# A written-out order of five engines replaced by another, with idle products at the beginning

## The chip, the cores and the metric

One core of a Trainium2 chip runs the kernel. The time is the device time of one execution in microseconds, here as the median of 11 runs. The core has a matrix engine (PE, with its weight loads shown apart as PEld), a vector engine (DVE), an activation engine (ACT), a general engine (POOL) and a queue engine (SP) that issues the large transfers. The engines run side by side, each through its own queue in order.

## The reference, cut to what matters

Four batches with 8 heads, 768 positions and 64 channels go through a decaying linear attention, and the result, as 3072 rows of 512, through a highway layer.

```python
for b in range(nb):                                  # blocks of 64 positions
    intra = np.einsum('bhic,bhjc->bhij', qb, kb) * Dmask[None]
    intra = np.einsum('bhij,bhjd->bhid', intra, vb)
    inter = np.einsum('bhid,bhde->bhie', qb * lam_pow[None], kv_state)
    out[:, :, sl] = intra + inter
    kv_state = lam_block * kv_state + np.einsum('bhsd,bhse->bhde', kb_dec, vb)
...
H = np.maximum(x @ w_h, 0.0)
T = 1.0 / (1.0 + np.exp(-(x @ w_t + b_t)))
return T * H + (1.0 - T) * x
```

## The kernel before, in words

The work is cut into 12 steps of 256 positions of one batch, numbered n = 0 to 11, three to a batch; each step has two halves b of 128 positions. The decay is put into q and v ahead of time (`pow_q`, `pow_v`), so that blocks of 128 positions need only a triangular mask, and the state `kv` stays in the accumulators of PE through the three steps of a batch.

Nothing is scheduled by a tool. `PLAN` is a string of tokens; each token calls one function of `DO` (line 350), and the functions issue their instructions in the order of the tokens. So the string sets the order of every engine's queue at once. After `@` stands the engine of a copy or scaling, after `=` the accumulator banks that a product writes. The tokens, with n the step:

- `Lq Lk Lv` (line 173, on SP): load of one half of the heads of q, k or v, a quarter MB each. `W.w.g` (line 178, SP): half of the weights w, half a MB. `WC` casts a quarter of a weight matrix.
- `CQ CK CV` (lines 191 and 105 or 103): scaling or cast of q, k, v to bf16. The last index is the half of the heads, or 2 for all of them.
- `TQ TK` (line 205, PE): eight transposes (four for one half of the heads). `EQ EK`: their copy to `qT` and `kT`.
- `S`, `U` and, woven together, `SS` (lines 217 and 222, PE): scores and the update of the state. The third index of `SS` is the half e. In the last step of a batch `SS.n.0` holds scores only. `M` (line 256, DVE): a mask of scores, four a step. `KE`: copy of the state to `ss`.
- `I` and `A` (lines 272 and 282, PE): output from the state and from the masked scores. `D`: its copy to `xT`.
- `F.i.u.w` (line 301, PE): products of token group i with half u of weight matrix w, eight matmuls of 256 columns. Groups 11 and 12 are the two halves of step 11, of 128 columns. `H` (line 306, DVE) and `G` (line 315, ACT) work on the two results, `X` (line 319, DVE) joins them.
- `R` (line 328, PE) turns the result back and adds x, `E` copies it out, `ST` (line 338, SP) stores it. `B` and `BC` transpose and copy the bias.
- `Z.r` (line 344): r products of the identity with itself into a bank that nobody reads. The plan before has none.

Buffers are named pools with a fixed number of turns (`BUFS`, line 64), and a load waits for the last reader of the buffer that it takes.

## Time and profile before

| | |
|---|---|
| median of 11 runs | 112.2 us (110.93 to 113.71) |
| the profiled execution, its own time | 111.49 us |
| its span, first to last instruction | 109.8 us |
| PE busy | 94.2 us, 86% of the span |
| DVE busy | 84.0 us, 77% |
| ACT busy | 65.8 us, 60% |
| POOL busy | 60.9 us, 55% |
| mean transfer rate over the span | 251 GB/s |

A line of a timeline shows the start, the length, the engine, the line of the kernel, the operation with its output and input, the count, and in brackets how long the engine had been idle and what released it. Several instructions of one line in a row are merged. A line of the chain of waits shows the start, the length and who held the chain. The busy time of PE is modelled at the ends of matmuls, so a share of 99% means that the next instruction always stood ready, not that the array was full.

### The profile page before, as it was taken

What the parts mean: (1) busy time and instruction counts of PE and PEld (TensorE: products, weight loads), DVE (VectorE), ACT (ScalarE), POOL (GpSimd) and SP (SyncE); (2) the same over time, 40 slices, a digit from 0 to 9 for tenths busy, and PEclk for the clock granted to TensorE, in tenths of its full rate; (3) what the DMA queues carried; (4) which work ended last, traced back from release to release, by engine and by line L of the source; (5) the groups of instructions that cost most, each with busy time, mean ns of one, the idle gap of its engine ahead of it and who ended that gap; (6) DMA issues with size and microseconds to landing.
All of it is one profiled execution on the core that took longest, in us unless ns stands there. A gap on an engine that the chain in (4) does not pass through costs nothing.

```text
span 109.8 us, 4558 instructions
## 1 busy us (share of the span) xinstructions
PE 94.2 (86%) x1969; PEld 82.6 (75%) x1969; DVE 84.0 (77%) x144; ACT 65.8 (60%) x120; POOL 60.9 (55%) x51
## 2 busy tenths in 40 slices
PE   0007887979999999999999999999999999999960
PEld 0005775848788888999978988888888888889950
DVE  0204796569795899799999899899989867867870
ACT  3581035622599947695346459619595739666970
POOL 6073797648489877979637679794638400000000
PEclk9999999999999999999999999999999999999999
DMA  0999999999999999999999999899985432020585
GB/s 4 267 293 288 290 295 327 322 321 322 281 275 305 288 282 298 283 294 317 318 319 304 301 294 314 272 349 323 308 264 198 155 122 75 0 96 0 188 309 178
DMA packets 43899, 27.55 MB, mean 251 GB/s; under 512 B 1764, under 2 KB 40936, under 8 KB 43880
## 3 DMA queue, kind: packets, MB, share of 16 engines
q1 hardware_dynamic: 43728, 27.27, 86.2%
q8 instruction: 15, 0.25, 1.0%
q14 instruction: 4, 0.03, 0.1%
q10 hardware_dynamic: 152, 0.01, 0.1%
HBM read 20.98 MB, written 6.29 MB: 248 GB/s over the span
## 4 chain that ended last, share of the span: by engine, by line
PE 51%; DMA 18%; SPq 14%; POOL 5%; DVE 5%; issue 2%; ACT 1%; DVEq 0%; POOLq 0%
PE bt L301 15%; SPq L173 13%; PE bh L301 12%; DMA kf<-in_k_dram 11%; DMA w_f<-in_moe_w_h_dram 7%; PE bx L328 6%; PE bs L217 5%; PE bo L282 3%; PE bktr L205 3%; POOL kb L105 3%; PE bo L272 3%; DVE hm L306 2%; PE bqtr L205 2%; POOL qb L191 2%; PE kv L222 1%
## 5 line engine op out<-in xcount | busy, mean ns | idle before, releaser
L301 PEld LDWEIGHTS <-w_b 128*128 128x128 bf16 x416 | 36.7, 98 | 5.8 <-POOL w_b L105 0.8
L256 DVE TENSOR_TENSOR m<-bs,tri 128x512 bf16<-128x512 f32 x48 | 31.0, 680 | 3.2 <-PE bs L217 2.9
L191 POOL TENSOR_TENSOR qb<-qf,pow_q 128x1024 bf16<-128x1024 f32 (+1 forms) x13 | 22.9, 1771 | 8.1 <-DMA qf<-in_q_dram 3.9
L315 ACT ACTIVATE bt<-bt,bt_col 128x256 f32<-128x256 f32 (+1 forms) x52 | 21.9, 430 | 8.4 <-PE bt L301 5.6
L301 PE MATMUL bh<-xT,w_b 128*128 128x256 bf16 (+1 forms) x208 | 24.6, 264 | 0.3 <-DVE w_b L105 0.3
L301 PE MATMUL bt<-xT,w_b 128*128 128x256 bf16 (+1 forms) x208 | 24.2, 265 | 0.1
L191 POOL TENSOR_TENSOR vs<-vf,pow_v 128x1024 bf16<-128x1024 f32 (+1 forms) x12 | 22.0, 1835 | 3.9 <-DMA vf<-in_v_dram 3.9
L319 DVE TENSOR_TENSOR th<-bt,hm 128x512 bf16<-128x512 f32 (+1 forms) x26 | 16.6, 644 | 2.9 <-ACT bt L315 2.0
L105 POOL CAST kb<-kf 128x1024 bf16<-128x1024 f32 (+1 forms) x12 | 12.0, 1003 | 10.8 <-DMA kf<-in_k_dram 8.3
L103 ACT ACTIVATE o<-bx 128x512 f32<-128x512 f32 x20 | 11.8, 597 | 9.2 <-PE bx L328 9.1
L306 DVE SCALAR_TENSOR_TENSOR hm<-bh,xT 128x512 bf16<-128x512 f32 (+1 forms) x26 | 16.2, 640 | 1.3 <-PE bh L301 1.3
L205 PE MATMUL bqtr<-id,qb 128*128 128x128 bf16 x96 | 8.2, 235 | 8.8 <-POOL qb L191 8.8
L217 PE MATMUL bs<-qT,kT 64*64 64x128 bf16 x384 | 14.6, 226 | 0.3 <-DVE qT L105 0.3
L217 PEld LDWEIGHTS <-kT 64*64 64x64 bf16 x384 | 11.4, 110 | 3.1 <-issue 2.1
L103 ACT ACTIVATE qT<-bqtr 128x1024 bf16<-128x1024 bf16 x9 | 9.2, 1027 | 7.6 <-PE bqtr L205 7.6
L205 PEld LDWEIGHTS <-qb 128*128 128x128 bf16 x96 | 6.2, 105 | 9.5 <-POOL qb L191 9.0
L328 PE MATMUL bx<-id,th 128*128 128x128 bf16 x96 | 12.9, 219 | 0.3 <-DVE th L319 0.3
L328 PE MATMUL bx<-id,xT 128*128 128x128 bf16 x96 | 12.9, 219 | 0.0
L103 ACT ACTIVATE xT<-bo 128x512 bf16<-128x512 f32 x13 | 9.2, 744 | 5.2 <-PE bo L282 5.2
L222 PE MATMUL kv<-vs,kb 64*64 64x64 bf16 x320 | 9.6, 201 | 0.9 <-ACT ss L103 0.8
L328 PEld LDWEIGHTS <-th 128*128 128x128 bf16 x96 | 9.4, 98 | 0.6 <-DVE th L319 0.5
L205 PE MATMUL bktr<-id,kb 128*128 128x128 bf16 x96 | 8.4, 235 | 1.4 <-POOL kb L105 1.3
(43 smaller groups left out, 102.6 us busy)
## 6 DMA issues: line engine op xcount, KB each, us to landing
qf<-in_q_dram SPq DMA_DIRECT2D x24, 256.0 KB, 5.2
kf<-in_k_dram SPq DMA_DIRECT2D x24, 256.0 KB, 5.5
vf<-in_v_dram SPq DMA_DIRECT2D x24, 256.0 KB, 5.5
out_dram<-o SPq DMA_DIRECT2D x23, 256.0 KB, 3.6
w_f<-in_moe_w_h_dram SPq DMA_DIRECT2D x2, 512.0 KB, 7.0
w_f<-in_moe_w_t_dram SPq DMA_DIRECT2D x2, 512.0 KB, 7.6
out_dram<-oh SPq DMA_DIRECT2D x2, 128.0 KB, 1.9
lam_bc<-in_lam_dram ACTq DMA_DIRECT2D x1, 4.0 KB, 3.5
```

Of the source, the lines that this page charges most:

```text
L103: A.activation(dst, src, AF.Copy)
L105: ENG[eng].tensor_copy(dst, src)
L173: nc.sync.dma_start(out=new((x + "f", n), [128, H, J * D], F32)[:, hs], in_=SRC[x][b, hs, c * 2 * C:(c + 1) * 2 * C, :].rearrange("h (p j) ...
L191: ENG[eng].tensor_tensor(dst, in0=get(src, n)[:, heads(p)].rearrange("p h (j d) -> p h j d", j=J), in1=pw[:, n % NST, heads(p), :, None].t ...
L205: T.transpose(t[:, i, j, :], get(x + "b", n)[:, j, h:h + 2, :], id128)
L217: T.matmul(get("s", n, e, hp // 2)[half(b), hp % 2, j, :], lhsT=get("kT", n)[half(e), hp, j, half(b)], rhs=get("qT", n)[half(e), hp, :, ha ...
L256: V.tensor_tensor(new(("m", n, e, u), [128, 2, J, C]), in0=get("s", n, e, u), in1=tri[:, None].to_broadcast([128, 2, J, C]), op=ALU.mult)
L301: T.matmul(t[:, r, :], lhsT=w_b[w][:, kc, (2 * u + r) * 128:(2 * u + r + 1) * 128], rhs=get("xT", *g)[:, kc, :], start=(kc == 0), stop=(kc ...
L306: V.scalar_tensor_tensor(new(("hm", g, u), [128, 2, z * C], tag=f"hm{z}"), in0=get("h", g, u), scalar=0.0, in1=get("xT", *g)[:, 2 * u:2 * ...
L315: A.activation(dst[:, r, :], src[:, r, :], AF.Sigmoid, bias=bt_col[:, 2 * u + r:2 * u + r + 1])
L319: ENG[eng].tensor_tensor(new(("th", g), [128, NP, z * C], tag=f"th{z}")[:, 2 * u:2 * u + 2, :], in0=get("tt", g, u), in1=get("hm", g, u), ...
L328: T.matmul(t[:, a * 128:(a + 1) * 128], lhsT=x[:, j, r * C:(r + 1) * C], rhs=id128, start=(a == 0 and i == 0), stop=(i == 1), skip_group_c ...
```

## The change

The string is replaced as a whole. The function `load` gets an argument for its queue; no token of the new string sets it. All work tokens are there as before; 55 of them have another engine, and nine `Z` tokens with 101 products in all are added. The start of the two strings:

```diff
-Lq.0.0 Lq.0.1 Lq.1.0 Lk.0.1 Lv.0.1 Lk.0.0 Lv.0.0 Lk.1.0 CQ.0.1@POOL Lq.1.1 Lv.1.1 CQ.0.0@POOL CK.0.1@ACT Lk.1.1
-TQ.0.0=0 TQ.0.1=1 Lv.1.0 TK.0.1=2 EK.0.1@DVE CK.0.0@POOL Lq.2.1 CV.0.1@DVE TK.0.0=3 EQ.0.1@DVE CV.0.0@POOL Lk.2.0
-EQ.0.0@DVE S.0.1=45 EK.0.0@DVE Lq.2.0 U.0.0 S.0.0=62 B=1 KE.0.0@DVE CQ.1.2@POOL W.0.1 M.0.1.0 U.0.1 M.0.0.1 Lk.2.1
-M.0.0.0 CK.1.2@POOL TQ.1.2=0 KE.0.1@DVE I.0=32 W.0.0 EQ.1.2@ACT CV.1.2@POOL TK.1.2=4 M.0.1.1 Lv.2.0 EK.1.2@DVE A.0.1
...
+Lk.0.0 Lk.0.1 Lk.1.0 Lq.0.0 Lv.0.0 Lv.0.1 Lq.0.1 Lk.1.1 Z.27=0 B=0 CK.0.1@ACT Lq.1.1 CK.0.0@ACT Z.2=1 TK.0.1=1 Lq.1.0
+TK.0.0=2 CQ.0.0@POOL Lv.1.1 EK.0.0@DVE BC CV.0.0@DVE Lv.1.0 Z.15=3 TQ.0.0=3 CV.0.1@DVE Lq.2.1 EQ.0.0@DVE Z.17=0 U.0.0
+CQ.0.1@POOL Lq.2.0 S.0.0=45 KE.0.0@DVE CK.1.2@ACT Lk.2.1 EK.0.1@DVE Z.9=0 U.0.1 M.0.1.0 TQ.0.1=6 Lk.2.0 TK.1.2=2
+M.0.0.0 EQ.0.1@ACT CQ.1.2@DVE W.0.1 EK.1.2@ACT Z.2=0 I.0=03 S.0.1=15 A.0.0 KE.0.1@ACT M.0.1.1 Z.4=4 TQ.1.2=6 Lv.2.0
+CV.1.2@DVE EQ.1.2@ACT W.1.1 M.0.0.1 Z.18=2 SS.1.1=42 CQ.2.2@POOL Lv.2.1 A.0.1 KE.1.0@ACT M.1.1.1 D.0.1@ACT M.1.1.0
+Z.7=1 SS.1.0=56 W.1.0 I.1=12 KE.1.1@ACT M.1.0.1 TQ.2.2=3 CK.2.2@ACT M.1.0.0 W.0.0 A.1.1 D.0.0@DVE A.1.0 WC.0.1.0@POOL
...
-    def load(x, n, p):
+    def load(x, n, p, eng):
...
-        nc.sync.dma_start(out=new((x + "f", n), [128, H, J * D], F32)[:, hs],
+        (A if eng else nc.sync).dma_start(out=new((x + "f", n), [128, H, J * D], F32)[:, hs],
```

In the order of each engine: K is loaded first instead of Q. CK of steps 0, 1 and 2 is on ACT; CQ.1.2 and all CV of steps 0 to 2 are on DVE; CQ of steps 0 and 2 stays on POOL. Of the weights, W.0.1 still comes first, then W.1.1, W.1.0 and W.0.0 (before: W.0.0, W.1.1, W.1.0). PE begins with Z.27 and has Z.15 and Z.17 ahead of TQ.0.0 and U.0.0, and runs the highway blocks of groups 0 and 1 in the order F.0.1.0, F.1.1.0, SS.2.0, F.0.1.1, F.1.1.1, SS.2.1, F.1.0.1, F.0.0.1 (before: F.0.1.0, F.0.0.0, F.1.1.0, F.1.0.0, SS.2.0, SS.2.1, F.0.1.1, F.1.1.1, F.0.0.1, F.1.0.1). On DVE the ramp reads EK.0.0, BC, CV.0.0, CV.0.1, EQ.0.0, KE.0.0, EK.0.1, M.0.1.0, M.0.0.0, CQ.1.2, M.0.1.1, CV.1.2, M.0.0.1, the four M of step 1, D.0.0, D.1.1, D.1.0, WC.1.1.1, H.1.1, CV.2.2; later come four masks, H.0.1, D.2.1, X.1.1, H.1.0, X.0.1, X.1.0, H.0.0, H.2.1, X.0.0, EQ.3.2. On ACT 15 of the 20 KE now stand (before 10). At the end E.10.0.2 and E.11.1.1 are on ACT instead of DVE.

## The prediction

> **What bounds the kernel now.** I read the busy table first, then busy time by stretches, the chain that ended last, and the timelines of the engines up to 29 us.

> ```profile
> span 109.8 us, 4558 instructions
> PE 94.2 (86%) x1969; PEld 82.6 (75%) x1969; DVE 84.0 (77%) x144; ACT 65.8 (60%) x120; POOL 60.9 (55%) x51
> ...
> PEclk9999999999999999999999999999999999999999
> ```
> ```profile
> 8.37:17.36 8.99, 7.48 (x129) 6.48 (x133) 6.34 (x12) 1.22 (x2) 6.44 (x5) 1.00 1.18 294
> 17.36:23.35 5.99, 4.50 (x144) 3.60 (x135) 3.21 (x8) 4.06 (x6) 3.95 (x4) 1.00 1.14 325
> 23.35:102.94 79.59, 79.00 (x1656) 69.62 (x1657) 70.32 (x115) 52.37 (x98) 46.59 (x31) 1.00 0.85 247
> 102.94:109.80 6.86, 3.26 (x56) 2.92 (x53) 3.23 (x8) 3.31 (x9) 0.00 (x0) 0.98 0.68 250
> ```

> The columns are stretch, length, then busy time of PE, its weight loads, DVE, ACT and POOL. From 23.35 PE is busy 79.0 of 79.6 us, so in that stretch PE's own work is the time and no new order can take much out. What can move is the ramp, 23.35 us that hold only about 8 us of PE work at full pace, and the tail, 6.86 us. DVE is second in the long stretch: 70.3 of 79.6 us, 88%.

> The ramp ends on a transfer. In the chain:

> ```profile
> 14.88 7.96 DMA w_f<-in_moe_w_h_dram
> 22.84 0.05 issue
> 22.90 0.88 POOL w_b L105
> 23.82 1.27 PE bh L301 x11
> ```

> The second block of weights lands at 22.8, is cast, and F.0.0.0 follows. Loads run in one queue, and the instructions that wait for them show the pace: the 4th load is used at 7.93 (CK.0.1 on ACT), the 6th at 9.77 (CK.0.0), the 9th at 12.44 (CQ.1.2), the 15th at 17.98 (CQ.2.2): 0.9 us per quarter MB, the n-th at 4.3 + 0.9n.

> PE is not at one speed, though the PEclk row never shows less than 9:

> ```profile
> 14.40 1.03 PE L205 MATMUL bqtr<-id,qb 128*128 128x128 bf16 x8 [0.47 <-POOL qb L191]
> 15.23 0.63 PE L272 MATMUL bo<-qT,ss 128*128 128x128 bf16 x4
> 15.65 1.06 PE L205 MATMUL bktr<-id,kb 128*128 128x128 bf16 x8
> 16.65 0.96 PE L282 MATMUL bo<-m,vs 64*64 64x128 bf16 x32
> ...
> 19.94 0.62 PE L205 MATMUL bqtr<-id,qb 128*128 128x128 bf16 x8
> ```

> The same eight transposes take 1.03 us at 14.40 and 0.62 at 19.94; less the 0.2 us of the last one's own time that is 107 ns apiece against 56. PE is slow until about 17.4, after 3.0 us of unbroken work since 14.40; it had begun steady work at 11.31, 6.1 us before, with a gap of 0.47.

> **The change, part by part.** The new argument of load() is empty in all 72 load tokens, so every load stays on SP. What changes is the order on each queue, the engine of 55 evacuations and casts, and 101 idle products.

> *Idle products.* Z.27 needs only id128, ready at 1.4: 27 x 107 ns = 2.9 us, 1.45 to 4.35. Real work can't start before ACT has loaded its tables (7.56) and cast K: CK.0.1 0.63 us, so TK.0.1 at 8.25 and TK.0.0 at 8.8 to 9.25. Z.15 then stands before TQ.0.0 and Z.17 before U.0.0. At the slow pace these are 1.6 and 1.8 us: TQ.0.0 ends at 11.3 instead of 9.7, U.0.0 starts at 13.1. At full pace throughout Z.17 would end at 11.3 (Z.15 to 10.1, TQ.0.0 to 10.35, Z.17 to 11.3), when U.0.0's own inputs are ready too. When does the pace double? The trace bounds it: after 3.0 us of unbroken work, so 8.25 + 3.0 = 11.3, or after 6.1, so 14.3. U.0.0 starts between 12.2 and 13.1; I take 12.7. Z.27 alone raising the pace for good would be the lower end, 11.3.

> *Casts moved.* POOL loses 9.5 us that nothing waits for late. DVE gains, all in the ramp, CV.0.0 (0.71, row L191 DVE), CQ.1.2, CV.1.2 and CV.2.2. DVE's 1024-wide form is not in the trace: by its 512 row doubled it is 1.43, by the step from 256 to 512 elements in the row of th (0.42 to 0.685) it is 0.685 + 2 x 0.263 = 1.21. I take 1.23, nearer the row of the same shape step. DVE loses KE, EK and D later, about the same amount in sum, so its total stays near 84 us; only the ramp is heavier.

> *The DVE chain in the ramp,* with 0.62 us from mask to mask (three masks in 1.88 us at 13.16), 0.35 for a 512-wide bf16 copy: U.0.0 12.7, KE.0.0 13.4 (0.44 for the products, 0.22 until DVE starts), EK.0.1 14.0, M.0.1.0 14.35, M.0.0.0 15.0, CQ.1.2 15.6, M.0.1.1 16.8, CV.1.2 17.4, M.0.0.1 18.6. Behind CQ.1.2 PE waits for TQ.1.2 (16.9), ACT for EQ.1.2 (to 18.55), and SS.1.1 for both it and CV.1.2 (18.65). SS.1.1 18.7 to 19.3, KE.1.0 on ACT to 20.1, SS.1.0 to 20.75, its masks on DVE 20.95 to 22.25, then D.0.0, D.1.1, D.1.0, 0.65 each, to 24.2. Before, those masks were done at 20.86, because Q and V of step 1 were scaled on POOL.

> *PE from there.* F.0.1.0 at 23.15 (WC.0.1.1 on ACT behind CK.2.2), F.1.1.0 at 24.25 behind D.1.0, 0.87 each (8 products of 109 ns); SS.2.0 to 25.5; F.0.1.1 and F.1.1.1 25.6 to 27.35; H.1.1 and CV.2.2 on DVE to 27.2; SS.2.1 to 28.05; F.1.0.1 at 28.1. The same work (four F blocks and both SS of step 2) was done before at 27.27, and then a wait of 0.3 for the third weight block followed, so the mark is 27.57. The ramp costs 28.1 - 27.57 = +0.5. All slow up to 13.9 it is +0.9 (U.0.0 at 13.1); all fast -0.6 (F.1.0.1 at 26.95: then V of step 2, which has 5.5 MB up to its end in both orders and was used at 24.75, ends last, with CV.2.2 to 26.05).

> *Weights.* W.0.1 comes 0.25 MB later (at 4.5 MB, about 20.9), W.1.1 0.75 MB earlier (about 23.8), W.1.0 0.75 MB earlier (about 26.1), W.0.0 1.5 MB later (about 27.9). In the chain above every one is there before its block; if DVE were faster, W.1.1 would hold F.0.1.1 until 24.5.

> *Long stretch.* PE's work is the same. DVE leaves the ramp with a queue: after CV.2.2 come masks 2, H.0.1, D.2.1, three X, H.1.0, H.0.0, H.2.1, X.0.0, some 10 us without a gap, before EQ.3.2. Laid against PE's row of blocks this costs 0.1 at F.2.1.1 (D.2.1) and 0.3 at SS.3.1 (EQ.3.2). The bounds are 0 and 1.5 (0.15 in each of ten further steps). Later transfers, laid on the same pace by bytes, are ahead of PE by over 1 us at each step, so I cost the new load and store order at nothing; without that cover a quarter MB late is 0.9. For the rest of the stretch I add 0.2, against 0.59 of idle now.

> *Tail.* E.10.0.2 and E.11.1.1 go to ACT, where the copy takes 0.38 to 0.60 against 0.42 to 0.68. The chain F.12.1.0, H, X, R, copy, store (104.5 to 109.8) keeps its links: H.12.1 starts at 105.18, when its block is done, not when DVE is free. Nothing.

> Sum: 0.5 + 0.4 + 0.2 = +1.1. Span 109.8 + 1.1 = 110.9; with the 1.69 around it (111.49 - 109.8), 112.6. The profiled run stood 0.7 under the median of 112.2, so the median is 113.3.

> [...]

> **Rivals.** *Pace up early, not slower:* Z.27 lifts the pace and the idle stretch up to 8.25 doesn't lose it, the ramp ends on transfers, -0.6, and DVE's queue hides: 111.6; with the 0.59 of idle gone too, 111.0. For it: PE did double after 3.0 us of work. Against it: 3.9 us with almost no work follow. It decides if U.0.0 starts before 11.6. *DVE becomes the bound:* late DVE work delays PE in every step, 0.9 + 0.4 + 1.5 = +2.8: 115.0. For it: 88% busy now; against: it has waits today for PE itself (2.2 us in masks) to give. *Nothing moves:* the ramp ends where the bytes do and PE's work is unchanged: 112.3. For it: V of step 2 at the same 5.5 MB; against: DVE's four extra scalings stand in the chain.

> **How the numbers follow.** Forecast 0.42, early pace 0.30, DVE bound 0.15, nothing moves 0.13. A measurement of this kernel tells about 1% from no change. Slower by more: over half of the forecast (0.25), the DVE case, 0.05 of the last, 0.45 in all. Faster by more: two thirds of the early case, 0.20. Within: 0.35. The likeliest case alone spans 112.2 to 114.2 (ramp 0.0 to +0.9, stalls 0 to 1.1); the range takes in both outer cases down to 111.0 and up to 114.9.

> **What would show it.** Right: Z.15 and Z.17 at 107 ns apiece, U.0.0 past 12, D.1.0 near 24, F.1.0.1 near 28, SS.3.1 waiting on qT from DVE. Wrong: 56 ns in Z.15; DVE idle for over a microsecond between 14 and 24; PE waiting for w_b or for DMA at 24 to 28; PE idle over 2 us after 28.

## The result and the profile after

The changed kernel takes 116.72 us (median of 12 runs, 113.88 to 118.05), the kernel before 112.29 us on the same chips (47 runs). The ratio is 1.025 [1.020, 1.030]: slower. The forecast was 113.3 us with a range up to 114.9, so the direction was right and the size wrong. Seven of the 12 runs, one at 115.60 and six from 117.84 to 118.05, are not in the ratio; the profiled run is one of the others, at 114.11 us, with a span of 112.3 against 109.8.

The page of the changed kernel, first the span and the busy times, then the granted clock (PEclk, the share of full clock that PE was given, in tenths) and the queue that brings the engines their instructions:

```profile
span 112.3 us, 4744 instructions
PE 100.3 (89%) x2070; PEld 88.6 (79%) x2070; DVE 86.4 (77%) x141; ACT 74.0 (66%) x131; POOL 50.8 (45%) x43
...
PEclk9995899999999999999999999999999999999997
...
q8 instruction: 16, 0.26, 1.0%
```

PE has 101 products and 101 weight loads more. The last line is 16 packets of 16 KB, which will matter below. Busy time by stretches (stretch, length, then PE, its loads, DVE, ACT, POOL, the granted clock, the DMA share and GB/s):

```profile
5.30:8.70 3.40, 0.09 (x1) 0.00 (x0) 0.66 (x2) 3.36 (x5) 0.58 (x1) 1.00 1.15 310
8.90:12.10 3.20, 3.13 (x28) 2.79 (x29) 2.02 (x4) 1.04 (x2) 1.65 (x2) 0.50 1.20 292
12.20:23.90 11.70, 10.36 (x290) 8.66 (x288) 10.72 (x15) 6.27 (x10) 2.51 (x2) 1.00 1.16 313
23.90:30.70 6.80, 5.51 (x99) 4.37 (x89) 4.68 (x8) 3.87 (x6) 1.46 (x3) 1.00 1.09 299
30.70:105.00 74.30, 74.29 (x1588) 66.63 (x1585) 65.10 (x106) 53.76 (x99) 42.54 (x27) 1.00 0.79 234
```

From 30.70 to 105 PE is busy without a gap. The loss lies ahead of it. Two places show it, the first on the timeline of DVE, POOL and PE:

```profile
15.77 1.21 DVE L192 TENSOR_TENSOR qb<-qf,pow_q 128x1024 bf16<-128x1024 f32 x1
...
17.50 2.57 DVE L192 TENSOR_TENSOR vs<-vf,pow_v 128x1024 bf16<-128x1024 f32 x1
20.00 2.09 DVE L257 TENSOR_TENSOR m<-bs,tri 128x512 bf16<-128x512 f32 x3
...
28.43 1.22 DVE L192 TENSOR_TENSOR vs<-vf,pow_v 128x1024 bf16<-128x1024 f32 x1
17.09 1.90 POOL L192 TENSOR_TENSOR qb<-qf,pow_q 128x1024 bf16<-128x1024 f32 x1 [5.02 <-DMA qf<-in_q_dram]
20.13 0.19 PE L223 MATMUL kv<-vs,kb 64*64 64x64 bf16 x1 [1.15 <-DVE vs L192]
```

In the kernel before, both stood on POOL, one after the other:

```profile
15.29 1.90 POOL L191 TENSOR_TENSOR vs<-vf,pow_v 128x1024 bf16<-128x1024 f32 x1
17.98 1.90 POOL L191 TENSOR_TENSOR qb<-qf,pow_q 128x1024 bf16<-128x1024 f32 x1 [0.79 <-DMA qf<-in_q_dram]
```

DVE's 1024-wide scaling takes 1.21 and 1.22 us, but CV.1.2 takes 2.57, and PE's SS.1.1 stands idle for 1.15 us waiting for it. CV.1.2 starts while POOL's CQ.2.2 runs (17.09 to 18.99) and ends 1.08 after that, so DVE got nowhere until POOL had finished. The chain of waits:

```profile
17.58 2.51 DVE vs L192
...
24.02 0.38 PE bktr L206 x5
24.41 1.29 issue
25.70 0.34 PE bktr L206 x3
```

The second loss: PE stops inside TK.2.2, five of eight transposes done, for 1.29 us, and the release is "issue", that is, nothing the profile shows as a wait. All inputs of the other three were there.

Where the 2.5 us of span come from: F.1.0.1 starts at 30.70 instead of 27.57, the mark of the prediction: +3.1. From there to the last H (H.12.1, before at 105.18, now at 107.23) it is 1.1 us shorter. The end is 0.5 longer: the last copy is done 3.3 us before the end of the span (108.99), before it was 2.8.

### The profile page after: what moved, and what is told of

Its sections match the earlier page's. It is cut to its first block, busy times and chain, and to the rows that moved or that the text cites. A ratio compares the mean times of both kernels' runs of the same rounds, so it can differ in the third digit from the quotient of the medians.

```text
span 112.3 us, 4744 instructions
## 1 busy us (share of the span) xinstructions
PE 100.3 (89%) x2070; PEld 88.6 (79%) x2070; DVE 86.4 (77%) x141; ACT 74.0 (66%) x131; POOL 50.8 (45%) x43
## 2 busy tenths in 40 slices
DMA packets 43900, 27.57 MB, mean 245 GB/s; under 512 B 1764, under 2 KB 40936, under 8 KB 43880
## 3 DMA queue, kind: packets, MB, share of 16 engines
q1 hardware_dynamic: 43728, 27.27, 83.6%
## 4 chain that ended last, share of the span: by engine, by line
PE 77%; ACT 6%; DVE 6%; issue 4%; DMA 4%; DVEq 0%; ACTq 0%
PE bt L302 18%; PE bh L302 18%; PE bx L329 9%; PE bs L218 8%; PE bo L283 6%; PE bktr L206 6%; PE bqtr L206 4%; PE bo L273 4%; DMA lam_bc<-in_lam_dram 4%; PE bspin L349 3%; PE kv L223 2%; DVE vs L192 2%; ACT o L104 2%; ACT bt L316 2%; DVE m L257 2%
## 5 line engine op out<-in xcount | busy, mean ns | idle before, releaser
L192 POOL TENSOR_TENSOR qb<-qf,pow_q 128x1024 bf16<-128x1024 f32 (+1 forms) x12 | 21.4, 1787 | 21.1 <-DMA qf<-in_q_dram 16.9
L192 POOL TENSOR_TENSOR vs<-vf,pow_v 128x1024 bf16<-128x1024 f32 x9 | 17.1, 1902 | 9.8 <-DMA vf<-in_v_dram 7.4
L104 ACT ACTIVATE kT<-bktr 128x1024 bf16<-128x1024 bf16 x9 | 9.1, 1025 | 5.2 <-PE bktr L206 5.2
L104 ACT ACTIVATE xT<-bo 128x512 bf16<-128x512 f32 x14 | 10.2, 749 | 3.3 <-PE bo L283 3.2
L104 ACT ACTIVATE ss<-kv 128x512 bf16<-128x512 f32 x15 | 8.9, 593 | 5.0 <-PE bs L218 4.2
L206 PE MATMUL bktr<-id,kb 128*128 128x128 bf16 x96 | 7.9, 227 | 4.8 <-ACT kb L104 3.5
L104 ACT ACTIVATE o<-bx 128x512 f32<-128x512 f32 x17 | 9.8, 596 | 3.2 <-PE bx L329 3.2
L104 ACT ACTIVATE qT<-bqtr 128x1024 bf16<-128x1024 bf16 (+1 forms) x8 | 7.7, 967 | 4.8 <-PE bqtr L206 4.8
L349 PE MATMUL bspin<-id 128*128 128x128 bf16 x101 | 9.5, 260 | 1.4 <-POOL id masks.py:199 1.4
L206 PEld LDWEIGHTS <-kb 128*128 128x128 bf16 x96 | 6.0, 100 | 5.9 <-ACT kb L104 4.0
```

Of the source, the lines that this page charges most:

```text
L104: A.activation(dst, src, AF.Copy)
L192: ENG[eng].tensor_tensor(dst, in0=get(src, n)[:, heads(p)].rearrange("p h (j d) -> p h j d", j=J), in1=pw[:, n % NST, heads(p), :, None].t ...
L206: T.transpose(t[:, i, j, :], get(x + "b", n)[:, j, h:h + 2, :], id128)
L349: T.matmul(t, lhsT=id128, rhs=id128, start=True, stop=True)
```

## The experiments

For (b) I counted PE's recorded instructions (products and weight loads) against the packets of the instruction queue. The trace of the kernel before has 15 such packets for 3938 recorded instructions, that of the changed one 16 for 4140, each of 16,384 bytes. The pieces end at number 193 + 256k: the standstills of the changed kernel, e2, e9 and e12 (705), e1 (1217), e13 (1729 and 2241) and e8 (3265) all lie within a few instructions of such a number. When PE crosses one end, the packet that it needs at the next end is sent, after a wait of 0 to 4.3 us (probably among the loads: in the changed kernel it is nothing from 87 us on, when the DMA engines have almost nothing to move); it takes about 1.1 us (0.88 to 1.59 in the kernels before and after). If PE reaches the next end before the packet is in, or soon after it, PE stands still until 1.3 to 1.7 us behind its arrival. In the stretch from 449 to 705 of the kernels that keep all 101 products, and of the kernel before:

```text
kernel       449 crossed  packet sent + took  705 reached  stood still
after           20.22        23.21 + 1.12        24.19        1.51
e2              18.35        21.32 + 1.15        22.21        1.54
e9              18.47        21.50 + 1.11        22.46        1.58
e12             20.12        24.22 + 1.11        23.98        2.83
before          21.37        24.10 + 1.10        29.45        0.11
```

(Starts of instructions, so the gaps are a little longer than the idle time in the timeline.) Before, PE needed 8.1 us for those 256 instructions; now the span between the ends holds the many small products of SS.1.0, Z.7, A.1.1 and TQ.2.2 and goes by in 4.0.

**No idle products (e1), and no moved casts either (e8).**

```diff
# e1: all nine Z tokens out
-... Z.27=0 ... Z.2=1 ... Z.15=3 ... Z.17=0 ... Z.9=0 ... Z.2=0 ... Z.4=4 ... Z.18=2 ... Z.7=1
# e8: also
-CK.0.0@ACT CK.1.2@ACT CK.2.2@ACT CQ.1.2@DVE CV.0.0@DVE CV.1.2@DVE CV.2.2@DVE
+CK.0.0@POOL CK.1.2@POOL CK.2.2@POOL CQ.1.2@POOL CV.0.0@POOL CV.1.2@POOL CV.2.2@POOL
```

> The changed plan without its nine Z tokens. Theory 1 (DVE's scaling of V in step 1 collides with POOL, and PE stands still 1.29 us inside TK.2.2 because the 202 instructions of the idle products have used up its supply): the standstill in TK.2.2 goes, U.0.0 starts up to 0.5 earlier, the scaling still takes 2.5: the profiled span goes from 112.3 to 110.5 to 111.2. Rival A (the DVE queue is long, collision or not, and the standstill has nothing to do with the idle products): span 111.8 to 112.3. Rival B (the idle products keep PE fast and are worth their time): without them PE is slow up to about 15 us, and the span is 112.8 or more.

> The changed plan without Z, and seven casts and scalings of steps 0 to 2 (CK.0.0, CK.1.2, CK.2.2, CQ.1.2, CV.0.0, CV.1.2, CV.2.2) back on POOL, where the kernel before has them: the new order alone. If the moved casts help the ramp by themselves (they start as soon as their loads land): F.1.0.1 later than the 27.16 of the plan without Z, by 0.3 to 0.8, as CV.2.2 on POOL takes 1.9 and not 1.2; span 109 to 110.3. If their collisions are what they cost: no scaling on DVE but one is left to collide, and the time is that of the kernel without Z or better.

e1: 111.78 us, ratio 0.997 [0.988, 1.007], span 109.7. e8: 111.51 us, 0.999 [0.993, 1.006], span 109.2. F.1.0.1 starts at 27.16 in both. The whole loss goes with the idle products, and without them the seven casts cost nothing. Timeline of e1, DVE, POOL and PE:

```profile
16.12 1.22 DVE L191 TENSOR_TENSOR vs<-vf,pow_v 128x1024 bf16<-128x1024 f32 x1
17.17 1.93 POOL L191 TENSOR_TENSOR qb<-qf,pow_q 128x1024 bf16<-128x1024 f32 x1 [5.09 <-DMA qf<-in_q_dram]
42.31 0.19 PE L222 MATMUL kv<-vs,kb 64*64 64x64 bf16 x1 [0.98 <-issue]
```

CV.1.2 was expected to keep its 2.5 us (span 110.5 to 111.2). But U.0.0 started at 10.63 instead of 13.15, CV.1.2 now begins before CQ.2.2, and it takes 1.22. So in the changed kernel it is the idle products that push CV.1.2 behind CQ.2.2. TK.2.2 is unbroken, but a standstill of the same kind appears at 41.1 (piece end 1217: 961 crossed at 36.16, packet at 39.60, 1217 reached at 41.11).

**The casts back on POOL, the idle products kept (e9).** The cast lines of e8 alone.

> The changed plan with all its idle products, and the same seven casts and scalings back on POOL. Theory 1 (collision 1.35, standstill 1.3, the rest from the idle products' own time): the collision goes, the standstill in TK.2.2 stays: span 110.6 to 111.4, F.1.0.1 near 28.7 to 29.3. Rival A (the DVE queue's length): the same, without a standstill it would be 110 or less. Rival B (the moved casts carry the plan): 112 or more.

112.77 us, ratio 1.013 [1.006, 1.021], span 110.7, F.1.0.1 at 29.05. The span and the start of F.1.0.1 are as expected: no 1024-wide scaling on DVE, and 1.65 us of the ramp back. The standstill stays:

```profile
22.23 0.45 PE L206 MATMUL bktr<-id,kb 128*128 128x128 bf16 x5
24.04 0.34 PE L206 MATMUL bktr<-id,kb 128*128 128x128 bf16 x3 [1.36 <-issue]
```

It falls after the fifth transpose again, with other engines' work around it: the place is given by the count.

**One cast moved back (e2).**

```diff
-CV.1.2@DVE
+CV.1.2@POOL
```

> One token of the changed plan: CV.1.2 on POOL instead of DVE, where POOL is idle from 12.1 to 17.1. Theory 1: POOL does it from 15.1 to 17.0 before CQ.2.2, DVE's M.0.0.1 comes 2.5 earlier, SS.1.1 waits only for qT on ACT (18.7) and starts 1.3 earlier than 20.1, and the end moves by 1.0 to 1.3. Rival A (DVE queue alone): DVE is relieved by 1.2 and the end by no more than 0.5. Rival C (the standstill of PE inside TK.2.2 ends at a time of its own): TK.2.2 still ends near 25.7 and the end moves by less than 0.3.

115.69 us (113.08 to 116.89), no ratio; the profiled run 113.08 with a span of 111.0. F.1.0.1 at 28.75, two microseconds earlier than in the changed kernel (0.53 of it from an earlier U.0.0). The exclusion works in the other direction as well:

```profile
15.23 1.21 DVE L192 TENSOR_TENSOR qb<-qf,pow_q 128x1024 bf16<-128x1024 f32 x1
15.42 2.79 POOL L192 TENSOR_TENSOR vs<-vf,pow_v 128x1024 bf16<-128x1024 f32 x1 [3.20 <-DMA vf<-in_v_dram]
```

POOL begins 0.19 after DVE and takes 2.79 instead of 1.90: it gets going when DVE is done at 16.44. The standstill in TK.2.2 stays here too (table above).

**The time without the number (e3), and that without the moved casts (e13).**

```diff
-Z.27=0 ... Z.15=3 ... Z.17=0 ...
+Z.7=0 ... Z.4=3 ... Z.4=0 ...        # 26 products in all
-            T.matmul(t, lhsT=id128, rhs=id128, start=True, stop=True)
+            T.matmul(t, lhsT=id128, rhs=wide, start=True, stop=True)   # wide: 128 x 512
# e13: with the cast lines of e8
```

> The changed plan with every idle product four times as wide (512 columns of a constant tile) and a quarter as many: 26 instead of 101, the same time on PE within 0.3 us, 150 instructions fewer. Theory 1: the standstill in TK.2.2 goes (PE reaches it with 150 instructions less behind it), the collision stays: the end moves by -1.0 to -1.3. Rival A or B: no change, within 0.3.

> The changed kernel with idle products of four times the width and a quarter of the number (26), and with the seven casts back on POOL: their time stays, their number and the moved casts go. Theory: neither the standstill (TK.2.2 unbroken) nor a scaling that DVE and POOL both want (DVE has no 1024-wide scaling); what stays is only the delay of U.0.0 to about 13; F.1.0.1 27.4 to 28.4, ratio 1.000 to 1.007. Rival (the delay of the first products by itself is what costs, and the order behind can't take it up): F.1.0.1 near 29, ratio 1.010 or more.

e3: 112.84 us, 1.010 [1.003, 1.018], F.1.0.1 at 29.69; no standstill in TK.2.2, but CV.1.2 still meets POOL's CQ.2.2 and takes 2.32. e13: 111.94 us, 1.000 [0.996, 1.005]. Its TK.2.2, on the timeline of PE:

```profile
21.53 0.62 PE L208 MATMUL bktr<-id,kb 128*128 128x128 bf16 x8
```

All eight in 0.62, and F.1.0.1 at 27.14, a little ahead of the 27.4 to 28.4 expected. So PE spends the same time on idle products, U.0.0 starts at 12.4, and nothing is lost: the rival, that their time costs by itself, is out. The profiled run of e13, 112.80 us, is near the upper end of its ten, and later in it PE waits twice for packets (0.56 and 0.29 us of idle time), at piece ends 1729 and 2241.

**The number without the time (e12).**

```diff
-        t = bank(("spin", idle[0]), bk[0], [128, 128])
+        t = bank(("spin", idle[0]), bk[0], [32, 32])
...
-            T.matmul(t, lhsT=id128, rhs=id128, start=True, stop=True)
+            T.matmul(t, lhsT=id128[:, 0:32], rhs=id128[:, 0:32], start=True, stop=True)
```

> The changed kernel with all nine Z tokens and their 101 products, each cut from 128x128x128 to 32 columns of weights by 32 moving columns: 29 ns apiece in the run that issued 80 of them, so the number of PE's instructions stays and most of their time goes (Z.15 and Z.17 together 0.9 us instead of 2.95). Theory (the number and the time of the idle products cost by two separate ways): U.0.0 near 11.5, CV.1.2 on DVE starts near 16.1, ahead of POOL's CQ.2.2, and takes 1.22; but the boundary of PE's instruction pieces still falls into TK.2.2, a standstill of 1.2 to 1.6 us there; F.1.0.1 at 28.2 to 28.8, span 110.6 to 111.4, ratio 1.005 to 1.015. Rival (only the time of the products costs, the standstill is due to something else): no standstill in TK.2.2, F.1.0.1 near 27.2, span near 109.7, ratio near 0.997.

116.56 us (4 runs, 114.3 to 118.11), ratio 1.030 [1.021, 1.038], from two of the four. The early U.0.0 and the standstill came as expected; the free CV.1.2 and the time did not (F.1.0.1 at 33.38, span 115.7, in a run of 118.11 us). Timeline of PE, DVE and POOL, and two stretches (the column after POOL is the granted clock):

```profile
23.75 0.45 PE L206 MATMUL bktr<-id,kb 128*128 128x128 bf16 x5
26.82 0.34 PE L206 MATMUL bktr<-id,kb 128*128 128x128 bf16 x3 [2.62 <-issue]
17.75 2.23 DVE L192 TENSOR_TENSOR vs<-vf,pow_v 128x1024 bf16<-128x1024 f32 x1
16.99 1.90 POOL L192 TENSOR_TENSOR qb<-qf,pow_q 128x1024 bf16<-128x1024 f32 x1 [5.08 <-DMA qf<-in_q_dram]
```

```profile
27.00:29.50 2.50, 2.50 (x19) 1.73 (x16) 0.00 (x0) 2.06 (x3) 0.62 (x1) 0.71 1.13 285
29.50:33.00 3.50, 3.50 (x50) 2.73 (x52) 3.02 (x4) 0.08 (x1) 2.43 (x1) 0.72 0.93 267
```

The standstill is there, after the fifth transpose, with products that took 32 to 39 ns each: the number alone is enough. The size of 2.62 is that of one execution, where the packet waited 4.1 us instead of 3; after it the granted clock fell to half for a part of the next 6 us. The collision, though, did not go. U.0.0 started at 11.54, early as expected, but then CV.0.1 on DVE met POOL's CQ.0.1 (both CV of step 0 took 2.13 us together instead of 1.28, as in the changed kernel, where Z.17 hid it) and M.0.1.1 waited for scores until 17.14. So my chain "idle products, late U.0.0, late CV.1.2" is one way into the collision and not the only one.

**Other counts, no work tokens changed (e5).** No Z tokens of the plan; 80 or 104 products of 32 columns ahead of the bias, to move the pieces by 160 or 208 instructions.

```diff
+Z.80=0    # e5_shift160, after the first loads; e5_shift208: Z.104=0
```

> The changed plan without its Z tokens, and 80 tiny idle products (32 by 32) at the very beginning, where PE has nothing to do until 8.3: 160 instructions that shift where PE's supply of 256 instructions at a time ends. Theory 1 (PE stands still when it gets through 256 instructions before the next 16 KB have come, 4.5 to 5.5 us after it began them): counted in the trace of the plan without Z, the shortest such stretch between 8 and 82 us is then 5.1 us instead of 4.0, so the standstill of 1.2 us at 41.1 is gone and the span is 108.4 to 109.2 against 109.7. Rival A (the standstills come from elsewhere): 109.7 or more, as the added products can only cost.

> The same with 104 tiny products, 208 instructions: by the same count the 256 instructions from 18.0 and those from 37.5 us take only 3.8 and 4.0 us. Theory 1: one or two standstills of 1 to 1.5 us there, span 110 to 112, though it differs from the kernel with 80 only by 24 products ahead of 8 us. Rival A: the same time as with 80, within 0.4.

The standstills were absent at 160, as expected. At 208, the expected ones didn't come: the first of the two stretches counted as short took 6.1 us; the second, up to the end at 43.04, took 3.92 us as counted, but the packet waited only 1.3 us and was in 1.49 ahead. So the pieces can be counted, while the wait of the packet can't. At 160 the time was missed, 114.51 us, 1.022 [1.015, 1.029], with a span of 112.9 against 108.4 to 109.2 expected. At 208 it is 113.55, 1.013 [1.007, 1.019]; the span of 110.0 lies in the expected 110 to 112, but not for the reason given. The loss is in the ramp: F.1.0.1 came at 30.77 and 28.81, against 27.16 in e1. In both the first transposes of K came late (8.92 and 8.95, in e11 at 8.37), and in the first CV.0.0 with CV.0.1 took 2.13. PE was also slow for longer: in the first up to 26.0 (eight transposes in 1.04 us at 25.02), in the second again from 20.5 to 23.8 (granted clock 0.50). How much each costs was not tried apart.

**The same 160 instructions later (e11), and four buffers instead of five (e10).** Both without the Z tokens of the plan.

```diff
# e11
+Z.80=3    # 32 columns each, ahead of TK.0.1
# e10
-kf=5, qf=5, vf=5
+kf=4, qf=4, vf=4
```

> The changed plan without Z, and 80 tiny idle products between the bias and the first transposes, at about 5 to 7.3 us, where PE is idle. In the kernel with the same 80 at 1.4 us the scale factors came 0.6 later on ACT, CV.0.1 then collided with POOL (2.13 for two scalings instead of 1.28), and PE's pace doubled only at 26.0. If those were a matter of the start at 1.4: first K cast at 7.6, scalings 1.28, pace doubled by 18, no standstill at 41, span 108.4 to 109.2. If idle products cost the ramp wherever they stand: 110.5 or more.

> The changed plan without Z, and four instead of five buffers each for loaded q, k and v: fewer loads stand in the queues at once. Theory 1 (the 16 KB of instructions wait 2 to 3.4 us behind loads): the waits shrink, the standstill of 1.2 us at 41 goes: span 108.3 to 109.2 against 109.7. Rival: PE waits for loads instead, 110 or more, and the instruction transfers wait as long as before.

e11: 112.67 us, 1.013 [1.004, 1.021], span 110.3, expected 108.4 to 109.2. Its ramp is as in e1 (F.1.0.1 at 27.31, CV of step 0 in 1.28), and there is no standstill at 41, so its loss lies later: the last store lands 1.4 us later than in most other runs. e10: 112.83 us (111.06 to 113.16), no ratio, span 111.0, expected 108.3 to 109.2. No standstill in it, and packets that waited 0 to 2.6 us instead of 0 to 3.4; but PE doubled its pace only at 25.4, and F.1.0.1 came at 29.83. It does not decide whether fewer loads in flight shorten the wait.

**Pace alone in the kernel before (e4).** Sixteen products of 512 columns ahead of TQ.0.0.

```diff
+Z.16=6    # 512 columns, in the plan of before, ahead of TQ.0.0
```

> The kernel before with 16 wide idle products ahead of its first transposes, from 1.5 us on: PE comes to its first work at the fast pace. Theory 1 and the forecast's view (the ramp of before ends when the second block of weights has landed, 22.84): no change within 0.3 us, though the eight first transposes take 0.62 instead of 1.03. Rival B (the pace in the ramp is what counts): faster by 0.8 or more.

112.51 us, 1.003 [0.993, 1.013]. Busy time by stretches:

```profile
5.30:12.10 6.80, 3.80 (x53) 2.08 (x53) 2.29 (x6) 2.93 (x5) 4.06 (x4) 1.00 1.20 293
12.10:18.90 6.80, 5.80 (x134) 5.18 (x129) 4.54 (x8) 1.91 (x3) 4.75 (x3) 0.50 1.17 306
```

PE was fast up to 12.1 and slow for the next 6.8 us, the reverse of the kernel before, and the time is the same. So it isn't PE's pace that ends the ramp of before; in the chain of waits it ends on a load.

**Two combinations (e6, e7).** e6 is e3 with CV.1.2 on POOL; e7 is the changed kernel without Z.15 and Z.17.

```diff
# e6
-CV.1.2@DVE
+CV.1.2@POOL          # and the wide products of e3
# e7
-Z.15=3
-Z.17=0
```

> The changed plan with wide idle products (a quarter as many, the same time on PE) and CV.1.2 on POOL: neither standstill nor collision, only the delay by the idle products' own time is left. Theory 1: F.1.0.1 starts 1.2 to 1.6 before the 29.7 of the wide kernel, span 109.3 to 109.8. Rival A (collision incidental): within 0.5 of 110.9.

> The changed plan without Z.15 and Z.17 alone (64 instructions fewer; Z.27 and the six small ones stay). Theory 1: U.0.0 starts about 1 to 1.5 us earlier, CV.1.2 on DVE starts before POOL's CQ.2.2 and takes 1.2, the standstill in TK.2.2 goes: span 108.5 to 109.8. Rival B (the idle products pay by the faster pace, and Z.27 cost the time): 111 or more.

e6: 112.26 us, 1.005 [1.002, 1.008], most of the loss gone. The profiled run is the longest of its twelve, 113.61 us, and missed what was expected (span 111.9, not 109.3 to 109.8; F.1.0.1 at 30.72, not 28.1 to 28.5): the granted clock was 0.50 from 19.1 to 22.4, and the scalings met in another pair. Timeline of DVE and POOL:

```profile
15.57 2.94 DVE L194 TENSOR_TENSOR qb<-qf,pow_q 128x1024 bf16<-128x1024 f32 x1
15.53 1.90 POOL L194 TENSOR_TENSOR vs<-vf,pow_v 128x1024 bf16<-128x1024 f32 x1 [3.23 <-DMA vf<-in_v_dram]
17.39 2.88 POOL L194 TENSOR_TENSOR qb<-qf,pow_q 128x1024 bf16<-128x1024 f32 x1
```

POOL begins 0.04 ahead of DVE and keeps its 1.90; DVE takes 2.94, and POOL's next scaling, which begins while DVE is at work, 2.88. e7: 113.85 us, 1.017 [1.013, 1.022], span 112.0, expected 108.5 to 109.8; the rival, that the idle products pay by their pace, had 111 or more. The standstill in TK.2.2 is gone, as its 64 instructions less move the piece ends; CV.0.0 with CV.0.1 took 2.13, CV.1.2 1.62, PE was slow up to 18.5 (granted clock 0.50 from 8.3 on), and F.1.0.1 came at 29.54. Which of these costs how much stays open.

The ratios side by side, by idle products and place of the seven casts:

| idle products | casts moved | casts on POOL |
|---|---|---|
| 101 of 128 columns | 1.025 [1.020, 1.030] | 1.013 [1.006, 1.021] (e9) |
| 101 of 32 columns | 1.030 [1.021, 1.038] (e12) | |
| 26 of 512 columns | 1.010 [1.003, 1.018] (e3) | 1.000 [0.996, 1.005] (e13) |
| none | 0.997 [0.988, 1.007] (e1) | 0.999 [0.993, 1.006] (e8) |

Down the left column, the step from 101 to 26 products is worth 1.5 to 2%. Across, the casts are worth about 1% as long as idle products stand in the ramp, and nothing without them. No version is clearly faster than the kernel before.

## Why the prediction was wrong

Up to CV.1.2 the ramp went as laid out; three terms of the sum were wrong: CV.1.2 was priced at 1.23 us and took 2.57; the idle products' instructions were put at nothing and cost 1.29; and the step from the profiled run to the median was put at 0.7 and measured 2.6. The first two are in the span, which grew by 2.5 us instead of 1.1: ramp +3.1 (forecast +0.5), long stretch -1.1 (+0.6), tail +0.5 (0). That the stretch went the other way hid part of the error of the ramp.

*Start of the ramp: a little late.* TK.0.1 came at 8.92 instead of 8.25, since ACT got to its cast of K only at 8.23. Z.15 ran at the slow pace as forecast (1.81 us for 15), Z.17 mostly at the full one (1.14). U.0.0 started at 13.15, forecast 12.7 in bounds up to 13.1. From there the chain caught up: M.0.1.0 14.58 (14.35), CQ.1.2 15.77 (15.6) and CV.1.2 17.50 (17.4) are within 0.25 us.

*The price of a 1024-wide scaling: right once, wrong where it counted.* 1.21 measured for CQ.1.2, 1.23 forecast. The term that failed is CV.1.2 at the same 1.23: it took 2.57, +1.34. The sum priced it by shape, with DVE alone, and laid out no timeline of POOL beside it, though the change leaves CQ.2.2 there at just that time. M.0.0.1 started at 20.0 instead of 18.6, and F.0.1.0 at 25.88 instead of 23.15. The runs show the size for these scalings: whoever begins second waits until the other is nearly done (DVE 2.57 here and 2.94 in e6, POOL 2.79 in e2 and 2.88 in e6). DVE's masks, which read one input from an accumulator bank, are not held up: in the changed kernel the 17 that had a scaling on POOL beside them for most of their time took 0.67 to 0.69 us, and so did the 17 with POOL idle.

*The idle products: their time was costed, their instructions were not.* This is the missing term, 1.29 us in TK.2.2. The forecast had PE go without a stop from D.1.0 to F.1.0.1. Shown by e9 and e12, which keep the number and the standstill, and by e3 and e13, which keep the time and lose it. The wait for the next piece is hidden here only while 256 instructions of PE last longer than the packet's wait and about 2.5 us (1.1 for the packet, about 1.4 behind it). In the kernel before the packet was never less than 1.88 us ahead.

Both together are 2.63 of the 2.6 us by which F.1.0.1 (30.70, forecast 28.1) was late; the earlier offset of 0.1 at CV.1.2 was taken up on the way. Without the collision F.1.0.1 came 1.65 us earlier (e9), without the standstill 1.01 (e3), without both 3.56 (e13), 0.74 of it from an earlier U.0.0. The ramp cost +3.1 against 0.5 forecast, bounds -0.6 to +0.9.

*The long stretch: wrong sign.* +0.6 was forecast. It was 1.1 us shorter: PE is busy 74.29 of 74.30 us from 30.70 to 105. In the kernel before there was 0.5 of idle time from 27.57 to 102.94:

```profile
27.57:102.94 75.37, 74.86 (x1583) 66.31 (x1582) 66.10 (x108) 51.74 (x97) 43.71 (x28) 1.00 0.84 243
```

The other half of the gain lies in PE's busy time for the same work. Of the two waits for DVE that the forecast had found, neither is there. From F.1.0.1 to H.12.1 the changed kernel took 76.53 us (before, from the mark, 77.61). In e11, with the same order, no standstill and a ramp that ended at 27.31, it took 76.89, so about 0.7 of the gain comes with the order. The other 0.4 is seen only where the ramp ended late: e2, e3 and e9 (F.1.0.1 at 28.75 to 29.69) took 76.5 with PE never idle, as if a late PE gave the other engines a lead.

*The tail: 0 forecast, +0.5 measured,* all of it after the last copy, in the landing of the last store, which varies by more than that between kernels with the same tail (2.9 to 4.3 us).

*From the profiled run to the median: 0.7 forecast, 2.6 measured.* The sum took the 0.7 over from the kernel before, as if the runs of the changed kernel would scatter alike. They scatter more: 113.88 to 118.05, before 110.93 to 113.71 (11 runs). With the span alone, +2.5 and 0.1 more around it, the forecast's own step would have given 114.8, inside its range; so 1.9 of the 3.4 us between 113.3 and 116.72 are this term. A scatter of 3.8 us came in e2 and e12 as well, which share with it the 101 products and CQ.1.2 on DVE, and in no other experiment more than 2.6. What the upper runs do differently stays open: no trace of the changed kernel shows one.

*The pace.* Z.27 ran slowly (3.06 us for 27), but the granted clock, 0.50 from 8.9 to 12.1, is shown as 1.00 in the stretch ahead of it (5.30 to 8.70), so the lift had come and was lost again, after 3.4 us in which PE was busy for 0.09 and before the first real product at 8.92. The forecast's 11.3 to 14.3 for the lasting rise held, at 12.1. The early-pace rival is out by this. Whether pace bounds the ramp at all, the prediction left open. For the kernel before, e4 shows that it doesn't. For the new order it may: without the plan's Z tokens F.1.0.1 came at 27.16 to 27.31 where PE doubled its pace at 17.0 to 17.4 (e1, e8, e11), and at 29.83 and 30.77 where it did at 25.4 and 26.0 (e10, e5 with 160). The pace does not explain the two losses above: e9 and the changed kernel doubled it at 12.3 and 12.1.

*The other rivals.* DVE as the bound gave 115.0, the nearest, for the wrong reason: DVE was late in the ramp alone. "Nothing moves" was right for the new order by itself (e1, e8), where the ramp ends at 27.16 against 27.27.

*Signs named beforehand.* Held: Z.15 at the slow pace, U.0.0 past 12. Not: Z.17 at the slow pace, D.1.0 near 24 (done at 25.4), F.1.0.1 near 28, SS.3.1 waiting for DVE. None of the four signs of a wrong forecast appeared either; DVE's standstill in CV.1.2 counts as busy time in the profile.

## What to carry to other kernels

An instruction moved to another engine is priced with what the neighbours do in the same microsecond: put such scalings of DVE and POOL on one timeline, as if they shared one engine (1.22 us became 2.57 here, 1.90 became 2.79 in e2). Work that fills gaps isn't free because the engine was idle: count its instructions as well as its time. Few wide ones cost 0 to 1% here (e13, e3) where many narrow ones cost 1 to 3% (e9, the changed kernel, e12). Part of that is where a piece happens to end: without any idle product (e1) a standstill of the same kind came at 41 us. When a profile shows "issue" in the middle of a run of equal instructions, look at the instruction packets and at the count since the last piece. And a step from one run to a median isn't carried over to a kernel whose scatter hasn't been measured.

## What was not expected of the hardware

The standstill of PE for want of instructions: from start to start 1.2 to 1.6 us in four kernels (e1, e2, e9 and the changed one) and 2.8 in e12, with the packet in 0.3 us before the end of the piece at most, or after it; with 0.9 to 1.1 us of lead 0 to 0.8 (e3, e8, e13), and with 1.3 or more never above 0.2. Behind the longest of them the granted clock was 0.71 (e12, 27.0 to 29.5). The exclusion of scalings: DVE 1.21 to 1.23 alone, 1.6 to 2.9 behind POOL; POOL 1.90 alone, 2.79 and 2.88 behind DVE. The instant at which PE's pace doubled for good went from 11.2 us (e13) to 26.0 (e5 with 160), and to 31.5 in e12, over kernels most of which issue much the same work in the ramp. Why is open, and so is the loss of e7 and, in part, of e5 and e11.
